# Where a check of the row sums stands in ScalarE's queue, and in which turns later pairs are transposed, in a routing-attention kernel with an MLP behind it

## The chip, the cores and the metric

The kernel runs on one core of a Trainium2 chip. The metric is the device time of one execution in microseconds (us). The kernel before has a median of 1115.66 us over three runs (1114.65 to 1117.67). The profile comes from one further execution of 1114.9 us, whose span from the first to the last instruction is 1113.0 us. PE is TensorE, DVE is VectorE, ACT is ScalarE, POOL is GpSimd, SP issues the DMAs.

## The reference

Four batches of eight heads, 768 positions, head size 64, everything in fp32. A query sees only those keys whose nearest centroid (of 16 for each head) is the same as its own. Then an MLP with a quick GELU over 3072 tokens.

```python
q_assign = argmax(einsum('bhsd,hcd->bhsc', q_n, c_n)); k_assign = ...
mask = q_assign[:, :, :, None] == k_assign[:, :, None, :]
scores = where(mask, scale * q @ k.T, -1e9)
attn = exp(scores - max);  attn = attn / (sum(attn) + 1e-9)
x = (attn @ v) as (B*S, H*D)
h = x @ w_in;  g = h * 1 / (1 + exp(-1.702 * h));  out = g @ w_out
```

## The kernel before, in words

Heads are worked in pairs, since two heads of 64 fill the 128 partitions: 16 pairs, numbered p, four in each batch. Queries are taken in halves of 384, so there are 32 groups g (a pair and a half), and each group has six units u, one for each block of 128 keys. The main loop runs over turns t, two units in a turn, 98 turns in all; three turns (TG) make a group, 24 (TB) a batch.

The order of the work on each engine is the order in which this loop emits it. There is no scheduler that reorders it: an engine takes its instructions one after another and waits at the first that isn't ready. One turn emits:

- `scores` (L392) of its two units on PE, into one of two PSUM buffers named `s`;
- `exps` (L417) on ACT. From the second batch on (turn 24) the result stays in `s`;
- `mask` (L428) on DVE, four instructions, which multiply by the comparison of the cluster codes and write `A`. They also set the `s` buffers free for the scores of the next turn. Then the row sums are added up on POOL (L438);
- `prep_near` (L284 on PE, L290 on ACT), if one is due, and then `values` (L449 on PE) of the turn before; behind a group's last unit ACT copies the result out (L454);
- in every third turn (t = 4, 7, 10, ...) a division, `normalise`: PE adds up the sums (L461), DVE takes the reciprocal (L464) and multiplies (L466). Such a turn is called a division turn here;
- the other steps of preparing a later pair (`prep_at` says in which turn): four transposes in steps 0 to 3 (L270 on PE, L275 on ACT), the nearest centroid, the assignment (L295 on PE, L301 to L324 on DVE), and the spreading of the codes (L331, L336 and two DMAs);
- `check`, two activations on ACT (L476 and L478), which read what the reciprocal wrote and keep two sums; a later test of these sums tells whether the fast path was allowed;
- pieces of the MLP, 0.62 of one in a turn for most of the loop (`first2`, L542, with a GELU at L485 and L486, or `second2`, L491). These fill PE while it would wait for attention.

PSUM has three buffers `m` for everything but scores and values: the transposes, L284, L295, L331, L461, and the MLP. An output of `second2` (`ys`) holds one of them for some eight pieces on end. Behind the loop PE works off the rest of the MLP, at L491 and L700.

Of the kernel before, what the change touches and what calls it, by code (L numbers as in the profile page):

```python
# [38 lines left out]
def fast(  # L39
# [111 lines left out]
    def load_w(i):  # L151
        if i < NW:
            t = wp.tile([P, WN, 2], I32, name="raw")
            nc.sync.dma_start(out=t.rearrange("p n t -> p (n t)"),
                              in_=w_chunks[i][1])
            w_raw[i] = t
# [5 lines left out]
    def split_w(i):  # L162

        hi = w_raw[i][:, :, 1]
        w = w_chunks[i][0]
        e = wp.tile([P, WN], I32, name="e", bufs=2)
        nc.vector.tensor_scalar(out=e, in0=hi, scalar1=EXP, scalar2=None,
                                op0=ALU.bitwise_and)
        nc.vector.tensor_scalar(out=w.bitcast(I32), in0=hi, scalar1=0xFFFFF,
                                scalar2=None, op0=ALU.bitwise_and)  # L170
        nc.scalar.activation(out=e, in_=e, func=AF.Relu, scale=8.0,
                             bias=low[:, 0:1])
        nc.scalar.activation(out=w, in_=w.bitcast(I32), func=AF.Copy,
                             scale=2.0 ** -20, bias=1.0)
        w_pow[i] = e

    def join_w(i):
        raw, e, w = w_raw.pop(i), w_pow.pop(i), w_chunks[i][0]
        nc.vector.scalar_tensor_tensor(
            out=e, in0=raw[:, :, 1], scalar=-2 ** 31, in1=e,  # L180
            op0=ALU.bitwise_and, op1=ALU.bitwise_or)
        nc.vector.scalar_tensor_tensor(
            out=w, in0=raw.bitcast(U32)[:, :, 0], scalar=2.0 ** -52, in1=w,
            op0=ALU.mult, op1=ALU.add)
        nc.vector.tensor_tensor(out=w, in0=w, in1=e.bitcast(FP32),
                                op=ALU.mult)
# [3 lines left out]
    def round_next():  # L190
        i = w_done[0]
        if i < NW:
            load_w(i + 2)
            split_w(i)
        if 0 < i <= NW:
            join_w(i - 1)
        w_done[0] += 1
# [188 lines left out]
    def scores(u):  # L386
        g, kt = divmod(u, NJ)
        p, h = split(g)
        ps = ps_s.tile([P, 2, 512], FP32, name="s")
        for a in range(2):  # L390
            rows = slice(a * D, (a + 1) * D)
            nc.tensor.matmul(out=ps[:, a, 0:HALF],  # L392
                             lhsT=T[p, 1][rows, kt * P:(kt + 1) * P],
                             rhs=T[p, 0][rows, h * HALF:(h + 1) * HALF],
                             start=True, stop=(p >= HP))
        s_of[u] = ps[:, :, 0:HALF]

    def part(u):

        g, kt = divmod(u, NJ)  # L400
        p, h = split(g)
        if p >= HP:
            return
        for a in range(2):
            r = 32 * (2 * (p % 2) + a)
            nc.tensor.matmul(
                out=s_of[u][:, a, :],
                lhsT=hots[p // 2, 1][r:r + NC, kt * P:(kt + 1) * P],
                rhs=hots[p // 2, 0][r:r + NC, h * HALF:(h + 1) * HALF],
                start=False, stop=True)  # L410

    def exps(u):
        p, h = split(u // NJ)
        s = s_of[u]
        if p < HP:
            A_of[u] = ap.tile([P, 2, HALF], FP32, name="A")
        nc.scalar.activation(out=A_of[u] if p < HP else s, in_=s, func=AF.Exp,  # L417
                             scale=SCALE)

    def mask(u):  # L420

        g, kt = divmod(u, NJ)
        p, h = split(g)
        s = s_of.pop(u)
        if p >= HP:
            A_of[u] = ap.tile([P, 2, HALF], FP32, name="A")
            for a in range(2):
                nc.vector.scalar_tensor_tensor(  # L428
                    out=A_of[u][:, a, :],
                    in0=qcode[p][:, a, h * HALF:(h + 1) * HALF],  # L430
                    scalar=code[p][:, kt % NH, 1, kt // NH, a:a + 1],
                    in1=s[:, a, :], op0=ALU.is_equal, op1=ALU.mult)
        A = A_of[u]
        if kt == 0:
            return
        if kt == 1:
            sum_of[g] = ap.tile([P, 2, HALF], FP32, name="sum", bufs=2)
        nc.gpsimd.tensor_tensor(out=sum_of[g],  # L438
                                in0=A_of[u - 1] if kt == 1 else sum_of[g],
                                in1=A, op=ALU.add)  # L440

    def values(u):
        g, kt = divmod(u, NJ)
        p, h = split(g)
        if kt == 0:
            o_of[g] = ps_o.tile([P, 512], FP32, name="o")
        A = A_of.pop(u)
        for a in range(2):
            nc.tensor.matmul(out=o_of[g][a * D:(a + 1) * D, 0:HALF],  # L449
                             lhsT=v_in[p][:, a, kt, :], rhs=A[:, a, :],  # L450
                             start=(kt == 0), stop=(kt == NJ - 1))
        if kt == NJ - 1:
            O_of[g] = xp.tile([P, HALF], FP32, name="x")
            nc.scalar.copy(O_of[g], o_of.pop(g)[:, 0:HALF])  # L454

    def normalise(g):

        sm = sum_of.pop(g)
        ps = bank()
        for a in range(2):  # L460
            nc.tensor.matmul(out=ps[a * D:(a + 1) * D, 0:HALF], lhsT=ones,  # L461
                             rhs=sm[:, a, :], start=True, stop=True)
        rec = recs[g] = short()
        nc.vector.reciprocal(out=rec, in_=ps[:, 0:HALF])  # L464
        x = xT_of[g] = O_of.pop(g)
        nc.vector.tensor_tensor(out=x, in0=x, in1=rec, op=ALU.mult)  # L466
        if g % HP == HP - 1 and g < 2 * HP:
            (half_ffn, ffn)[g // HP].extend((ffn_half, ffn_tiles)[g // HP]())

    recs = {}  # L470

    def check(g):


        rec = recs.pop(g)
        nc.scalar.activation(out=rec, in_=rec, func=AF.Copy,  # L476
                             accum_out=sums[:, 0, g:g + 1])
        nc.scalar.activation(out=rec, in_=rec, func=AF.Relu, bias=top[:, 0:1],  # L478
                             scale=-2.0 * LIMIT * LIMIT,
                             accum_out=sums[:, 1, g:g + 1])  # L480
# [85 lines left out]
    TG = NJ // 2  # L566
    TB = 2 * HP * TG

    prep_at = {}
    for p in range(1, NPAIR):  # L570
        b, hp = divmod(p, HP)
        for i in range(2 if p == 1 else 0, len(PREP)):
            if p == 1:
                t = (i - 2) // 2
            elif b == 0:
                t = (hp - 2) * TG + 1 + i // 2
            else:
                t = b * TB + (-8, -5, -2, 1)[hp] + i
            prep_at.setdefault(t, []).append((p, i))
    loads = deque((p, w) for p in range(NPAIR) for w in range(2))  # L580
    for _ in range(3):
# [2 lines left out]
    def prep(p, i):  # L584
        if i == 0 and p:
            load_v(p)
        PREP[i](p)
        if i in (1, 3) and loads:
            load_qk(*loads.popleft())
# [7 lines left out]
    for t in range(NT + 2):  # L597
        us = range(2 * t, 2 * t + 2) if t < NT else ()
        for u in us:
            scores(u)  # L600
        if t == 0:
            prep(0, 6)
        for u in us:
            part(u)
        for u in us:
            exps(u)
        second_half = t >= TB // 2
        if second_half:
            round_next()
        for u in us:  # L610
            mask(u)
        work = sorted(prep_at.get(t, ()), key=lambda w: PREP[w[1]] != prep_near)
        while work and PREP[work[0][1]] == prep_near:
            prep(*work.pop(0))
        if 1 <= t <= NT:
            for u in range(2 * t - 2, 2 * t):
                values(u)

        todo = half_ffn or (ffn if len(ffn) > NF // 2 else ())
        owed += (rate if half_ffn else 0.62) if todo else -owed  # L620
        g = (t - 2) // TG if t >= 2 and (t - 2) % TG == TG - 1 else None
        if g is not None and second_half:
            normalise(g)
        for p, i in work:
            prep(p, i)
        if g is not None and not second_half:
            normalise(g)
        if recs:
            check(*recs)
        if second_half or t and t % 4 != 3:  # L630
            round_next()
        while owed >= 1 and todo:
            todo.popleft()()
            owed -= 1
        if second_half and t % 2:
            round_next()
    qcode.clear()
    att.close()

# [561 lines left out]
```

## Time and profile before

| | us |
|---|---|
| median of three runs (1114.65 to 1117.67) | 1115.66 |
| profiled execution | 1114.9 |
| its span | 1113.0 |
| PE busy | 1039.0 (93%) |
| DVE busy | 603.0 (54%) |
| ACT busy | 359.5 (32%) |
| POOL busy | 295.9 (27%) |

The span falls into three stretches: batch 0 up to about 227 us, batches 1 to 3 (turns 24 to 97) up to about 633 us, and then the rest of the MLP. In the last stretch, from 633 to 1113, PE is busy for 474.24 of 480 us. "Idle" in a row is the time for which the engine stood still just before the instruction, and the arrow names what it waited for. A matmul in fp32 shows up as two instructions in the profile, so four matmuls of the kernel are x8 there.

### The profile page before, as it was taken

The page shows a single profiled execution, that of the slowest core. Times are in us where ns is not written, and L with a number is a line of the kernel's source. Part 1 is how long each engine was busy: PE and PEld are TensorE (multiplying, and loading weights), DVE is VectorE, ACT ScalarE, POOL GpSimd, SP SyncE. Part 2 cuts the span into 40 slices and gives each one's busy share as a digit, 9 for nine tenths or more (in the row PEclk, how much of TensorE's full clock was granted, in tenths as well). Part 3 has the DMA queues.
Part 4 walks back from the last instruction along what each step waited for, and adds up shares of the span by engine and source line. Part 5 has one row for each costly group of instructions (what it writes and reads, how often), then busy time and mean ns, then how long its engine had stood idle before and what let it go on. Part 6 is the DMA issues. An engine that isn't in the chain of part 4 may idle for free. (4 is left out here: it accounts for less than half of the span.)

```text
span 1113.0 us, 11101 instructions
## 1 busy us (share of the span) xinstructions
PE 1039.0 (93%) x4142; PEld 503.9 (45%) x4142; DVE 603.0 (54%) x912; ACT 359.5 (32%) x649; POOL 295.9 (27%) x168
## 2 busy tenths in 40 slices
PE   7878799999899998999897899999999999999997
PEld 4323354445434354444453355544455444555443
DVE  3889998237666786677776676600166300465000
ACT  4654555224435544554453212200022100122000
POOL 2554231215465555655565300000000000000000
PEclk9989899999989999999998999999999999999999
DMA  7423443211002310131000000000000000000000
GB/s 202 126 75 96 145 143 105 60 45 46 8 15 57 95 42 3 29 92 39 8 1 0 1 10 0 1 19 19 19 0 1 10 19 19 9 1 1 20 19 21
DMA packets 64816, 45.17 MB, mean 41 GB/s; under 512 B 51952, under 2 KB 57584, under 8 KB 64752
## 3 DMA queue, kind: packets, MB, share of 16 engines
q1 hardware_dynamic: 64608, 44.33, 13.9%
q8 instruction: 35, 0.57, 0.2%
q14 instruction: 29, 0.24, 0.1%
q10 hardware_dynamic: 144, 0.03, 0.0%
HBM read 38.04 MB, written 6.31 MB: 40 GB/s over the span
## 5 line engine op out<-in xcount | busy, mean ns | idle before, releaser
L438 POOL TENSOR_TENSOR sum<-sum,A 128x768 f32<-128x768 f32 x128 | 235.7, 1841 | 252.3 <-DVE A L428 153.4
L491 PE MATMUL m<-w_out,gb 128*128 128x512 f32 x576 | 247.7, 592 | 0.0
L428 DVE SCALAR_TENSOR_TENSOR A<-qb,code,s 128x384 f32<-128x384 uint8 x288 | 158.3, 610 | 125.5 <-ACT s L417 109.7
L705 DVE TENSOR_TENSOR gb<-b,gb 128x384 f32<-128x384 f32 x168 | 93.4, 557 | 213.8 <-PE b L700 207.2
L392 PE MATMUL s<-T,T 64*128 64x384 f32 x768 | 165.3, 542 | 35.6 <-DVE A L428 21.1
L491 PEld LDWEIGHTS m<-w_out,gb 128*128 128x128 f32 x576 | 109.4, 190 | 137.1 <-issue 136.6
L449 PE MATMUL o<-A,inv 128*64 128x384 f32 x768 | 154.1, 523 | 3.6 <-DVE A L428 3.6
L417 ACT ACTIVATE s<-s 128x768 f32<-128x768 f32 x144 | 109.5, 788 | 58.8 <-PE s L392 57.2
L392 PEld LDWEIGHTS s<-T,T 64*128 64x128 f32 x768 | 68.0, 195 | 113.5 <-issue 38.3
L496 ACT ACTIVATE y<-m 128x512 f32<-128x512 f32 x24 | 14.3, 597 | 257.0 <-PE m L491 243.9
L485 ACT ACTIVATE th<-gb 128x768 f32<-128x768 f32 x48 | 40.4, 843 | 170.1 <-DVE gb L705 140.3
L449 PEld LDWEIGHTS o<-A,inv 128*64 128x64 f32 x768 | 49.1, 142 | 94.0 <-issue 87.9
L464 DVE RECIPROCAL short<-m 128x384 f32<-128x384 f32 x32 | 81.7, 2552 | 12.7 <-PE m L461 12.7
L438 POOL TENSOR_TENSOR sum<-A 128x768 f32<-128x768 f32 x32 | 58.8, 1839 | 77.9 <-ACT A L417 41.7
L700 PE MATMUL b<-x,S 128*128 128x384 f32 x192 | 69.8, 486 | 0.0
L700 PE MATMUL b<-T,w_in 128*128 128x384 f32 x192 | 69.8, 486 | 0.0
L700 PE MATMUL b<-x,w_in 128*128 128x384 f32 x192 | 66.3, 486 | 0.0
L513 PE MATMUL m<-x,w_in 128*128 128x384 f32 x128 | 49.6, 543 | 13.3 <-ACT T L275 4.5
L486 DVE SCALAR_TENSOR_TENSOR gb<-th,gb 128x768 f32<-128x768 f32 x48 | 45.8, 954 | 21.8 <-ACT th L485 21.8
L491 PE MATMUL m<-w_out,g 128*128 128x512 f32 x120 | 56.8, 597 | 0.0
L542 PEld LDWEIGHTS m<-x,w_in 128*128 128x128 f32 x384 | 44.7, 192 | 10.7 <-issue 10.6
L476 ACT ACTIVATE short<-short 128x384 f32<-128x384 f32 x32 | 16.7, 523 | 100.8 <-DVE x L466 100.8
(95 smaller groups left out, 898.5 us busy)
## 6 DMA issues: line engine op xcount, KB each, us to landing
raw<-in_moe_w_in_dram SPq DMA_DIRECT2D x16, 512.0 KB
raw<-in_moe_w_out_dram SPq DMA_DIRECT2D x16, 512.0 KB
in<-in_q_dram SPq DMA_DIRECT2D x32, 192.0 KB
in<-in_k_dram SPq DMA_DIRECT2D x32, 192.0 KB
inv<-in_v_dram SPq DMA_DIRECT2D x16, 384.0 KB
out_dram<-y SPq DMA_DIRECT2D x24, 256.0 KB
qb<-line SPq DMA_DIRECT2D x12, 192.0 KB
line<-row SPq DMA_DIRECT2D x12, 1.5 KB
```

The costliest lines, as they stand in the source:

```text
L392: nc.tensor.matmul(out=ps[:, a, 0:HALF], lhsT=T[p, 1][rows, kt * P:(kt + 1) * P], rhs=T[p, 0][rows, h * HALF:(h + 1) * HALF], start=True, ...
L417: nc.scalar.activation(out=A_of[u] if p < HP else s, in_=s, func=AF.Exp, scale=SCALE)
L428: nc.vector.scalar_tensor_tensor(out=A_of[u][:, a, :], in0=qcode[p][:, a, h * HALF:(h + 1) * HALF], scalar=code[p][:, kt % NH, 1, kt // NH ...
L438: nc.gpsimd.tensor_tensor(out=sum_of[g], in0=A_of[u - 1] if kt == 1 else sum_of[g], in1=A, op=ALU.add)
L449: nc.tensor.matmul(out=o_of[g][a * D:(a + 1) * D, 0:HALF], lhsT=v_in[p][:, a, kt, :], rhs=A[:, a, :], start=(kt == 0), stop=(kt == NJ - 1))
L464: nc.vector.reciprocal(out=rec, in_=ps[:, 0:HALF])
L486: nc.vector.scalar_tensor_tensor(out=g, in0=t, scalar=1.0, in1=h, op0=ALU.add, op1=ALU.mult)
L491: nc.tensor.matmul(out=ps[:, 0:DM], lhsT=g, rhs=w_out[:, f, :], start=(f == 0), stop=(f == NF - 1))
L513: nc.tensor.matmul(out=ps[:, 0:HALF], lhsT=w_in[:, c, f * P:(f + 1) * P], rhs=xT[c], start=(c == 0), stop=(c == NCH - 1))
L542: nc.tensor.matmul(out=ps[:, f % 2 * P:(f % 2 + 1) * P], lhsT=w_in[:, c, f * P:(f + 1) * P], rhs=xT[c][:, n * P:(n + 1) * P], start=(c == ...
L700: nc.tensor.matmul(out=ps[:, 0:HALF], lhsT=a(c), rhs=x(c), start=(c == 0), stop=(c == 1))
L705: nc.vector.tensor_tensor(out=o, in0=a, in1=b, op=ALU.add)
```

## The change

Two things, both by place alone; no instruction is added or taken away. From turn 24 the check of a division turn is not emitted at the end of that turn but in the next turn, between `exps` and `mask`; the last one stands behind the loop. And the transposes of the pairs of batches 1 to 3 move: for a pair whose first group starts in turn T they stood in turns T-8, T-7, T-6 and T-5, one each, of which T-8 and T-5 are division turns; now there are two in T-7 and two in T-6. The other three steps stay in T-4, T-3 and T-2.

```diff
@@ -575,7 +575,7 @@
             elif b == 0:
                 t = (hp - 2) * TG + 1 + i // 2
             else:
-                t = b * TB + (-8, -5, -2, 1)[hp] + i
+                t = b * TB + TG * hp - (7, 7, 6, 6, 4, 3, 2)[i]
             prep_at.setdefault(t, []).append((p, i))
@@ -607,6 +607,8 @@
         if second_half:
             round_next()
+        if recs:
+            check(*recs)
         for u in us:
             mask(u)
@@ -625,7 +627,7 @@
         if g is not None and not second_half:
             normalise(g)
-        if recs:
+        if recs and t < TB:
             check(*recs)
@@ -634,6 +636,7 @@
         if second_half and t % 2:
             round_next()
+    check(*recs)
     qcode.clear()
     att.close()
```

ACT's queue in a division turn of batch 1, and in the two turns behind it, where no transposes are due (L417 is `exps`, L485 the GELU of an MLP piece, L454 the copy of a group's result). Before:

```order
L476 ACTIVATE short,sums<-short 128x384
L478 ACTIVATE short,sums<-short,top 128x384
L417 ACTIVATE s<-s 128x2x384 x2
L485 ACTIVATE g<-m 128x256
L417 ACTIVATE s<-s 128x2x384 x2
L454 COPY x<-o 128x384
L485 ACTIVATE g<-m 128x256
```

The same place now:

```order
L417 ACTIVATE s<-s 128x2x384 x2
L476 ACTIVATE short,sums<-short 128x384
L478 ACTIVATE short,sums<-short,top 128x384
L485 ACTIVATE g<-m 128x256
L417 ACTIVATE s<-s 128x2x384 x2
L454 COPY x<-o 128x384
L485 ACTIVATE g<-m 128x256
```

The two rows of the check have moved behind one pair of `exps`; what stands behind them is as it was.

PE's queue from a division turn on (its L461 to the first L491), through the next turn and the one behind that, where a pair is being prepared. Before:

```order
L461 MATMUL m<-sum,ones 64x384 x2
L331 LDWEIGHTS qc
L331 MATMUL m<-ident_h,qc 12x128
L270 MATMUL m<-ident,in 128x128 x6
L491 MATMUL m<-w_out,g 128x512 x2
L392 MATMUL s<-T_1666,T_1767 128x384 x4
L284 MATMUL m<-T_2318,cT 32x384 x2
L284 MATMUL m<-T_2398,cT 32x384 x2
L449 MATMUL o<-A,inv 64x384 x4
L270 MATMUL m<-ident,in 128x128 x3
L392 MATMUL s<-T_2213,T_2275 128x384 x4
L449 MATMUL o<-A,inv 64x384 x4
```

The same place now, from L331 to the second turn's transposes:

```order
L331 LDWEIGHTS qc
L331 MATMUL m<-ident_h,qc 12x128
L491 MATMUL m<-w_out,g 128x512 x2
L392 MATMUL s<-T_1706,T_1767 128x384 x4
L284 MATMUL m<-T_2349,cT 32x384 x2
L284 MATMUL m<-T_2398,cT 32x384 x2
L449 MATMUL o<-A,inv 64x384 x4
L270 MATMUL m<-ident,in 128x128 x6
L392 MATMUL s<-T_2237,T_2275 128x384 x4
L449 MATMUL o<-A,inv 64x384 x4
L295 MATMUL m<-ident,short 128x128 x3
L270 MATMUL m<-ident,in 128x128 x6
```

The two steps of transposes (x3 each) that stood behind L331 are gone from the division turn; the next two turns have two steps each instead of one, the second pair of them behind L295.

## Rows read from the trace of the kernel before

**Rows 1.** The page, busy time of each engine (share of the span) and instructions.

```profile
PE 1039.0 (93%) x4142; PEld 503.9 (45%) x4142; DVE 603.0 (54%) x912; ACT 359.5 (32%) x649; POOL 295.9 (27%) x168
```

**Rows 2.** Who PE waited for, 227 to 633 us: total, times, longest.

```profile
PE s L392 <- DVE A L428: 21.1, 11, 4.2
PE m L270 <- ACT T L275: 4.0, 7, 0.6
PE o L449 <- DVE A L428: 3.6, 1, 3.6
PE s L392 <- ACT g L485: 2.1, 3, 0.8
PE m L270 <- ACT row L336: 1.7, 5, 0.3
```

**Rows 3.** Groups of instructions, 227 to 623 us: busy, mean ns, idle before.

```profile
L476 ACT ACTIVATE short<-short 128x384 f32<-128x384 f32 x24 | 12.6, 523 | 73.7 <-DVE x L466 73.7
...
L478 ACT ACTIVATE short<-short,top 128x384 f32<-128x384 f32 x24 | 14.8, 615 | 0.8
```

**Rows 4.** Timeline of one division and the turns behind it: start, duration, idle before.

```profile
413.73 1.56 PE L392 MATMUL s<-T,T 64*128 64x384 f32 x8
...
414.02 2.55 DVE L464 RECIPROCAL short<-m 128x384 f32<-128x384 f32 x1
...
416.60 0.71 DVE L466 TENSOR_TENSOR x<-x,short 128x384 f32<-128x384 f32 x1
...
416.66 2.05 PE L542 MATMUL m<-x,w_in 128*128 128x128 f32 x16
417.35 0.52 ACT L476 ACTIVATE short<-short 128x384 f32<-128x384 f32 x1 [3.25 <-DVE x L466]
...
418.61 1.48 ACT L417 ACTIVATE s<-s 128x768 f32<-128x768 f32 x2
419.50 2.19 DVE L428 SCALAR_TENSOR_TENSOR A<-qb,code,s 128x384 f32<-128x384 uint8 x4 [2.19 <-ACT s L417]
...
420.78 1.97 PE L392 MATMUL s<-T,T 64*128 64x384 f32 x8 [2.07 <-DVE A L428]
...
426.10 1.56 PE L392 MATMUL s<-T,T 64*128 64x384 f32 x8
```

**Rows 5.** Timeline of PE, 264 to 300 us.

```profile
288.25 2.48 PE L392 MATMUL s<-T,T 64*128 64x384 f32 x8 [2.21 <-DVE A L428]
...
295.21 1.56 PE L392 MATMUL s<-T,T 64*128 64x384 f32 x8
```

**Rows 6.** PE's granted clock (behind POOL) in two stretches of it.

```profile
290.80:294.50 3.70, 3.70 (x19) 1.89 (x20) 1.61 (x3) 1.27 (x2) 2.65 (x2) 0.71 0.00 0
294.50:299.00 4.50, 4.50 (x29) 2.27 (x30) 2.30 (x5) 1.88 (x3) 0.90 (x2) 1.00 0.01 2
```

**Rows 7.** Timeline of two late turns without MLP pieces.

```profile
607.79 2.93 PE L392 MATMUL s<-T,T 64*128 64x384 f32 x8 [4.18 <-DVE A L428]
...
623.77 3.35 PE L449 MATMUL o<-A,inv 128*64 128x384 f32 x8 [3.57 <-DVE A L428]
```

**Rows 8.** Timeline of two turns without an MLP piece between their scores.

```profile
436.88 1.97 PE L392 MATMUL s<-T,T 64*128 64x384 f32 x8 [2.19 <-DVE A L428]
...
440.22 1.81 PE L392 MATMUL s<-T,T 64*128 64x384 f32 x8
```

**Rows 9.** Timeline of a division turn with transposes, and the turn behind it.

```profile
490.04 0.55 PE L270 MATMUL m<-ident,in 128*128 128x128 f32 x3 [0.34 <-ACT row L336]
...
491.15 0.55 PE L270 MATMUL m<-ident,in 128*128 128x128 f32 x3 [0.57 <-ACT T L275]
...
495.92 0.48 ACT L290 COPY short<-m 128x384 f32<-128x384 f32 x1
...
497.06 0.55 PE L270 MATMUL m<-ident,in 128*128 128x128 f32 x3
```

## The prediction

> **What bounds the kernel now.** I read the page first: PE is busy for 93% of the span, the other engines for a third to a half [rows 1]. So only PE's idle time is to be had, and whatever slows its clock. The view of the chain that ended last is of no use here: it ends in the last output's copy and is one step long. The second view was who PE waited for while attention of batches 1 to 3 runs: the largest entries are scores (L392) that wait for masks (L428), 21.1 us in 11 waits, then values (L449) that wait for masks, 3.6 in one wait, transposes (L270), 4.0 and 1.7, and scores behind a GELU, 2.1 [rows 2]. The third view, groups of instructions, shows ACT standing for 73.7 us in 24 waits at the check's first activation, each time until DVE's multiplication L466 is through [rows 3]. ACT has time enough, so this wait costs only by what is queued behind it, and the timeline shows that.
>
> In the turn of 414 us DVE takes the reciprocal from 414.02 to 416.57 and multiplies to 417.31 [rows 4]. PE issued the scores of the next turn at 413.73, 1.56 us, and they were done by 415.3. But ACT's next instruction is the check: it waits 3.25 us, runs from 417.35, and only at 418.61 do the exponentials of those scores begin. The masks follow at 419.50, after DVE has stood for 2.19 us. PE ends its MLP piece at 416.66 + 2.05 = 418.71 and stands for 2.07 us until the first mask has freed an `s` buffer; the next scores start at 420.78. So in a division turn a check that nobody needs soon holds back exponentials, masks and scores.
>
> **The check.** Behind the change the exponentials are ahead of the check. Their scores are ready at 415.3, and two of them take 1.48 us [rows 4], so they end at about 416.9, while DVE is still at the multiplication. The masks can start when DVE is free, at 417.35 instead of 419.50: 2.15 us earlier. The next scores could then start at 420.78 - 2.15 = 418.63, and PE comes to them at 418.71: the stall of 2.07 is gone, and what is late next is PE itself.
>
> How much of each stall goes is the smaller of the stall and 2.15. The three entries that the check causes add up to 21.1 + 3.6 + 2.1 = 26.8 us [rows 2]; the GELU one belongs to them since that GELU stands behind the check in ACT's queue. Two stalls are longer: 4.18 at 607.79 keeps 2.03, and 3.57 at 623.77 keeps 1.42, both late in the loop where no MLP piece is left [rows 7]. A few others lie slightly over 2.15, such as the 2.21 at 288.25 [rows 5]; I put these at 0.35 in all. Term 1: 26.8 - 2.03 - 1.42 - 0.35 = 23.0 us.
>
> Behind such a stall the pair of scores takes 1.97 instead of 1.56 us, because its second unit waits for a mask of its own [rows 4]. There are 14 such scores (11 and 3 waits, rows 2). I take half, since in turns without an MLP piece the loop of scores, exponentials and masks sets the pace anyway: 440.22 - 436.88 = 3.34 us from scores to scores [rows 8], and that stays. Term 2: 7 x 0.41 = 2.9 us (bounds 0 and 14 x 0.41 = 5.7).
>
> The check itself, 418.61 - 417.35 = 1.26 us, costs nothing if it is done before the next exponentials are due. It starts at 417.35 as before, once L466 is through; the next scores start at 418.7 and take some 0.8 for a unit, so the exponentials are due at 419.6, a microsecond after the check's end. Queued behind the check are now the copies of L284 and of transposes, the GELU of that turn's piece and those exponentials. If that cover went, it would cost up to 1.26 us in each of 24 turns, 30 us. The check of the last group moves behind the loop, with nothing late behind it: 0.
>
> **PE's clock.** The stall of 2.21 us at 288.25 is followed by a stretch of a granted clock of 0.71 on the mean, from 290.8 to 294.5, and then 1.00 again [rows 6]: for part of that stretch the lower level, 1.2 GHz. From these scores to the next, with an MLP piece between, it took 295.21 - 288.25 = 6.96 us [rows 5]; the same distance without a fall took 426.10 - 420.78 = 5.32 [rows 4]. A fall costs 1.64 us. I count seven falls, the first at 288.25 and the last at 623.77; five follow stalls that should vanish, two follow the late ones that only shrink. Upper bound 7 x 1.64 = 11.5, lower bound 0 (falls that come anyway, from the waits that are left). Five would give 8.2; I take term 3 as 6.
>
> The Trainium skill (TensorE: Matmul & The Clock Gate, section What's actually happening) says that the throttled clock is the default and activity lifts it; by that a vanished stall takes its fall along, 8.2 us, and without it the term would be 0. The trace agrees only in part: the stall of 2.07 at 420.78 had no fall behind it [rows 4].
>
> **The transposes.** Twelve pairs have them moved. In a division turn with `ys` held and the division's sums in a second buffer, one `m` buffer is left: the first transposes wait 0.34 for the copy of L331's result, the second 0.57 for the copy of the first [rows 9]. In total 1.7 and 4.0 us [rows 2]. The 0.34 goes, since L331 is alone now. The 0.57 recurs: in the turn of L295 its buffer is kept by DVE, `ys` by PE, and two transposes share one buffer again. In the turn ahead, the second transposes wait for L284's copy, which stands behind exponentials and check together, as before, and ends at 495.92 + 0.48 = 496.40; PE comes there at about 497.06 - 0.91 + 0.49 = 496.64, so no wait [rows 9]. On SP's queue the loads that steps 0 and 3 issue move by a turn with them: the values' load to one turn later, the next load of q to one turn earlier and so ahead of the codes' two DMAs (L338, L340). Each is needed three or more turns later, and no wait in rows 2 names a DMA, so I put this at nothing; held-up codes would stop the masks at a pair's start. Term 4: 1 us of gain. Bounds: 5.7 gained, or, if all 24 second transposes wait 0.57, 13.7 - 5.7 = 8 lost.
>
> The Trainium skill (Perfetto Trace Analysis, section Optimization Strategy) holds that a gap that repeats can mean too little PSUM for the next tile. By that rule moving them would give nothing, as long as there are three buffers; I lean that way, the 0.34 apart.
>
> **The sum.** 23.0 + 2.9 + 6 + 1 = 32.9 us. Against the profiled execution: 1114.9 - 32.9 = 1082.0. The median shown is 0.8 above that execution, so 1083.
>
> **The rivals.**
> *The clock does not come back.* The stalls go, but short waits still bring as many falls: 1083 + 6 = 1089. For it: not every stall has a fall, so what sets them off isn't the stall alone.
> *The next limit is near.* Half of terms 1 to 3 comes back as other waits, because DVE now goes from multiplication to masks without a pause and the 3.34 us loop governs more turns [rows 8]: 1083 + 16 = 1099. Against it: in most turns an MLP piece of 2 us stands on PE and covers the loop.
> *It does not do what it says.* DVE or POOL would have held the masks anyway: 1115. Against it: DVE's 2.19 of idle time ends with the exponentials [rows 4].
> *Slower.* ACT, now held at the check while copies stand behind it, delays the copies of two transposes in one turn, so that PE waits at each of 24 second transposes for the check and a copy, 1.26 + 0.57 = 1.83 us, 44 in all: 1083 + 44 = 1127. It decides from 1.4 us each, where 24 waits eat the 33 us. Against it: the copy's place worked out above.
>
> **Chances.** Forecast 0.60 (its own range 1076 to 1088), clock 0.12, next limit 0.17, no effect 0.06, slower 0.05. A difference of under 0.3% (3.3 us) can't be told from no change here; so faster 0.89, same 0.06, slower 0.05. The range leaves out the two last and half of the next limit, and at the low end what lies beyond some 40 us: 1075 to 1099.
>
> **What would show it.** In the profile after: no wait of scores for masks of about 2 us behind an MLP piece, and L417 ahead of L476 in each division; ACT's wait at L476 shorter than 73.7 us; masks that start right behind L466; granted clock 1.00 from 280 to 600 us; the span of batches 1 to 3 some 33 us shorter and the stretch behind it as long as before. Wrong would be a new wait of L270 or L295 for ACT of over 10 us, or scores that now wait as long for exponentials.

## The result, and the profile after

The changed kernel takes 1081.95 us, the median of four runs (1081.31 to 1083.81), against 1115.27 before on the same chip (four runs, 1114.65 to 1117.67): a ratio of 0.970 with a 95% interval of 0.968 to 0.972. The prediction was 1083. The profiled execution took 1083.81 us with a span of 1082.0, against 1114.9 and 1113.0.

The page of the kernel after, the row that answers to [rows 1]:

```profile
PE 1030.4 (95%) x4142; PEld 503.5 (47%) x4142; DVE 600.2 (55%) x912; ACT 359.6 (33%) x649; POOL 295.6 (27%) x168
```

No engine has less to do: the instructions are as many as before, and of the busy times only PE's is shorter by much, 8.6 us, since its matmuls run less often at the lower clock. The other 22 of the 31 us were idle time of PE.

Who PE waited for after, 220 to 603 us (total, times, longest):

```profile
PE m L270 <- ACT T L275: 2.8, 5, 0.6
PE m L461 <- POOL sum L438: 2.2, 1, 2.2
PE s L392 <- DVE A L428: 2.2, 3, 1.7
PE m L270 <- ACT short L290: 1.1, 1, 1.1
PE o L449 <- DVE A L428: 1.1, 1, 1.1
```

Against [rows 2] the scores' wait for masks has gone from 21.1 to 2.2 us, that of the values from 3.6 to 1.1, and the scores' wait behind a GELU is not there any more. One entry is new, the 1.1 us of transposes (L270) behind L290's copy. At the end of the loop PE's sums (L461) wait 2.2 us for POOL; that wait stood in the kernel before too, as the entry that follows the five of [rows 2] (227 to 633 us):

```profile
PE m L461 <- POOL sum L438: 1.3, 1, 1.3
```

ACT's own wait at the check is still there, but short (groups of instructions, 220 to 600 us: busy, mean ns, idle before; [rows 3] had 73.7):

```profile
L476 ACT ACTIVATE short<-short 128x384 f32<-128x384 f32 x24 | 12.6, 524 | 12.9 <-DVE x L466 12.9
```

One division of the kernel after, to be laid beside [rows 4] (start, duration, idle before):

```profile
401.59 1.56 PE L392 MATMUL s<-T,T 64*128 64x384 f32 x8
...
402.01 2.55 DVE L464 RECIPROCAL short<-m 128x384 f32<-128x384 f32 x1
...
402.60 1.50 ACT L417 ACTIVATE s<-s 128x768 f32<-128x768 f32 x2 [0.65 <-PE s L392]
...
404.52 2.05 PE L542 MATMUL m<-x,w_in 128*128 128x128 f32 x16
404.59 0.71 DVE L466 TENSOR_TENSOR x<-x,short 128x384 f32<-128x384 f32 x1
405.22 2.17 DVE L428 SCALAR_TENSOR_TENSOR A<-qb,code,s 128x384 f32<-128x384 uint8 x4
405.33 0.52 ACT L476 ACTIVATE short<-short 128x384 f32<-128x384 f32 x1 [1.23 <-DVE x L466]
...
406.50 1.96 PE L392 MATMUL s<-T,T 64*128 64x384 f32 x8
```

The exponentials (L417) run while DVE still takes the reciprocal, the masks start with the end of the multiplication (405.22, where L466 ends at 405.30), and PE goes from the MLP piece to the next scores without standing. Before, 4.12 us lay between the starts of L542 and of these scores (416.66 to 420.78); now 1.98. The scores still take 1.96 us, though nothing holds their start.

A window of the kernel after (its length; busy time of PE, PEld, DVE, ACT, POOL; granted clock, share of DMA, GB/s):

```profile
227.00:600.00 373.00, 360.95 (x1989) 172.72 (x1988) 275.42 (x418) 186.45 (x352) 217.33 (x120) 1.00 0.14 36
```

From 227 to 600 us PE is busy for 97% at a granted clock of 1.00 on the mean; before it was busy for 91% of 227 to 633 us, at 0.97 (a fall, below, is a stretch in which the granted clock is 0.50, the lower of its two levels):

```profile
227.00:633.00 406.00, 370.73 (x1983) 174.34 (x1980) 277.72 (x419) 186.02 (x352) 217.41 (x120) 0.97 0.13 33
```

A finer measure than the whole time is the distance from one group's reciprocal (L464) to the next, since each group has one. In groups 0 to 5 (batch 0) these distances differ by up to 5 us in sum between executions of one and the same kernel; from group 7 on they repeat to a few hundredths nearly everywhere. From group 7's reciprocal to group 31's it was 629.33 - 240.57 = 388.76 us before and 596.79 - 244.58 = 352.21 after: 36.6 us gained. Of that 4.0 are lost up to group 7's (244.58 against 240.57; group 6 alone took 42.51 instead of 37.77) and 1.5 behind group 31's, which leaves the 31.0 by which the span fell. So the change contains a loss, in batch 0's last turns. Group 6's own length shows it best: in a second execution of the changed kernel group 7's reciprocal came at 240.41, by the spread of the groups ahead, but group 6 took 42.27 again. The experiments take it apart.

### The profile page after: what moved, and what is told of

Same layout as the page of the kernel before. It is cut to its first block, busy times and chain, and to the rows that moved or that the text cites. A ratio compares the mean times of both kernels' runs of the same rounds, so it can differ in the third digit from the quotient of the medians.

```text
span 1082.0 us, 11138 instructions
## 1 busy us (share of the span) xinstructions
PE 1030.4 (95%) x4142; PEld 503.5 (47%) x4142; DVE 600.2 (55%) x912; ACT 359.6 (33%) x649; POOL 295.6 (27%) x168
## 3 DMA queue, kind: packets, MB, share of 16 engines
q1 hardware_dynamic: 64608, 44.33, 14.3%
## 5 line engine op out<-in xcount | busy, mean ns | idle before, releaser
L491 PE MATMUL m<-w_out,gb 128*128 128x512 f32 x576 | 247.7, 592 | 0.0
L491 PEld LDWEIGHTS m<-w_out,gb 128*128 128x128 f32 x576 | 109.4, 190 | 137.1 <-issue 136.6
L392 PE MATMUL s<-T,T 64*128 64x384 f32 x768 | 159.2, 527 | 13.1 <-ACT A L417 9.0
L449 PE MATMUL o<-A,inv 128*64 128x384 f32 x768 | 148.3, 506 | 1.1 <-DVE A L428 1.1
L417 ACT ACTIVATE s<-s 128x768 f32<-128x768 f32 x144 | 109.3, 793 | 83.2 <-PE s L392 72.0
L496 ACT ACTIVATE y<-m 128x512 f32<-128x512 f32 x24 | 14.3, 596 | 261.9 <-PE m L491 238.9
L485 ACT ACTIVATE th<-gb 128x768 f32<-128x768 f32 x48 | 40.4, 842 | 170.0 <-DVE gb L708 140.0
L464 DVE RECIPROCAL short<-m 128x384 f32<-128x384 f32 x32 | 81.7, 2552 | 14.7 <-PE m L461 14.6
L491 PE MATMUL m<-w_out,g 128*128 128x512 f32 x120 | 59.0, 616 | 0.2 <-ACT T L275 0.2
L542 PEld LDWEIGHTS m<-x,w_in 128*128 128x128 f32 x384 | 44.7, 192 | 11.2 <-issue 10.2
L542 PE MATMUL m<-x,w_in 128*128 128x128 f32 x384 | 48.8, 280 | 0.5 <-ACT T L275 0.5
```

The source lines that it names most:

```text
L392: nc.tensor.matmul(out=ps[:, a, 0:HALF], lhsT=T[p, 1][rows, kt * P:(kt + 1) * P], rhs=T[p, 0][rows, h * HALF:(h + 1) * HALF], start=True, ...
L449: nc.tensor.matmul(out=o_of[g][a * D:(a + 1) * D, 0:HALF], lhsT=v_in[p][:, a, kt, :], rhs=A[:, a, :], start=(kt == 0), stop=(kt == NJ - 1))
L491: nc.tensor.matmul(out=ps[:, 0:DM], lhsT=g, rhs=w_out[:, f, :], start=(f == 0), stop=(f == NF - 1))
L542: nc.tensor.matmul(out=ps[:, f % 2 * P:(f % 2 + 1) * P], lhsT=w_in[:, c, f * P:(f + 1) * P], rhs=xT[c][:, n * P:(n + 1) * P], start=(c == ...
```

## The experiments

A time is a median with its lowest and highest run; "group 6" is the distance from group 5's reciprocal to group 6's, and "loop" that from group 7's to group 31's, both in the profiled execution. The kernel before took 1114.56, 1115.44 and 1115.34 us in the three sessions (8 to 11 runs each), beside the first four experiments, the next four and the last three.

| kernel | us | ratio, 95% interval | group 6 | loop |
|---|---|---|---|---|
| before | | | 37.77 | 388.76 |
| changed | 1081.95 (1081.31 to 1083.81) | 0.970 (0.968 to 0.972) | 42.51 | 352.21 |
| check alone | 1080.38 (1079.22 to 1081.22) | 0.970 (0.968 to 0.971) | 37.73 | 353.57 |
| transposes alone | 1124.63 (1123.23 to 1125.17) | 1.009 (1.007 to 1.011) | 42.30 | 394.42 |
| batch 1's pairs at their old turns | 1076.40 (1076.15 to 1081.28) | 0.968 (0.966 to 0.970) | 37.73 | 353.79 |
| check of the group before | 1081.29 (1079.16 to 1083.24) | 0.971 (0.969 to 0.972) | 37.73 | 355.73 |
| check behind the reciprocal | 1095.96 (1093.41 to 1099.29) | 0.983 (0.981 to 0.986) | 37.74 | 371.72 |
| check at the next turn's end | 1078.73 (1074.73 to 1080.69) | 0.967 (0.965 to 0.969) | 37.74 | 352.86 |
| no check | 1077.02 (1072.93 to 1079.65) | 0.965 (0.963 to 0.967) | 37.74 | 353.02 |
| before, its stalls filled | 1103.46 (1101.86 to 1104.87) | 0.990 (0.988 to 0.992) | 37.73 | 378.93 |
| checks behind exponentials from turn 12 | 1081.04 (1080.09 to 1082.90) | 0.970 (0.968 to 0.971) | 38.58 | 353.23 |
| changed, again | 1081.68 (1079.19 to 1084.21) | 0.970 (0.968 to 0.972) | 42.27 | 352.47 |
| batch 1's at old turns, again | 1078.49 (1076.56 to 1081.15) | 0.966 (0.964 to 0.968) | 37.75 | 353.41 |

### The two parts apart

Check alone: the changed kernel with the transposes where they were.

```diff
-                t = b * TB + TG * hp - (7, 7, 6, 6, 4, 3, 2)[i]
+                t = b * TB + (-8, -5, -2, 1)[hp] + i
```

> The check moved, the transposes where they were before. Theory (the wait in ACT's queue is the whole gain): about 1080 us, so even slightly under the changed kernel's 1082, since the changed kernel lost some 4 us in batch 0 between 164 and 207 us, where only transposes moved, and won back 2 us at most by them later. Rival (the division turn was overloaded, the transposes did a good part): 1095 us or more.

Transposes alone: the same edit the other way round, in the kernel before.

> The transposes moved, the check where it was before. Theory: 1117 us or so, the 4 us of batch 0 lost and 1 to 2 us of waits for L331's copy won. Rival (transposes did a good part): 1100 us or less.

The check brings 1114.56 - 1080.38 = 34.2 us, more than the whole change. The transposes alone cost 10.1 us. Neither expectation had that number: the waits cost far more than was put on them. The view of PE's waits of this kernel, 120 to 633 us, shows where:

```profile
PE s L392 <- DVE A L428: 22.8, 13, 4.2
PE m L270 <- ACT short L290: 5.4, 5, 2.6
PE m L513 <- DVE short L464: 5.4, 1, 5.4
PE m L513 <- ACT short L290: 4.9, 1, 4.9
```

The rows with L290 add up to 10.3 us; in the kernel before PE waits for L290 once in this window, 2.2 us. One of these waits, on the timeline of the same kernel:

```profile
517.79 0.52 ACT L476 ACTIVATE short<-short 128x384 f32<-128x384 f32 x1 [3.26 <-DVE x L466]
...
519.05 1.48 ACT L417 ACTIVATE s<-s 128x768 f32<-128x768 f32 x2
...
520.46 0.48 ACT L290 COPY short<-m 128x384 f32<-128x384 f32 x1
...
521.00 0.90 PE L270 MATMUL m<-ident,in 128*128 128x128 f32 x3 [2.56 <-ACT short L290]
```

The second transposes of a turn need the buffer that L290's copy empties, and that copy stands behind the check and the exponentials. So the two parts depend on each other: with the check moved, four of the five waits in the loop are gone and the fifth is 1.1 us.

### Batch 1's pairs at their old turns

```diff
+            elif b == 1:
+                t = b * TB + (-8, -5, -2, 1)[hp] + i
             else:
                 t = b * TB + TG * hp - (7, 7, 6, 6, 4, 3, 2)[i]
```

> The changed kernel, but the four pairs of batch 1, whose transposes fall into the last turns of batch 0, keep their old turns. Theory (the 4.9 us wait at 179 us comes from two transposes in one turn whose PSUM buffers wait for a copy that ACT does late): 1078 us, and the reciprocals of groups 5 to 7 stand where they stood before. Rival (that stretch varies from run to run, or the check does it): 1082 us as with the change.

1076.40 us, and 1078.49 in another session beside the changed kernel's 1081.68. That repeat was to show 3 to 5 us with intervals that don't meet; it shows 3.2, and the intervals overlap at the edge. The traces are plainer. Group 6 takes 37.73 us again, not 42.51. The changed kernel's timeline shows what that group's turns hold:

```profile
173.65 0.87 PE L270 MATMUL m<-ident,in 128*128 128x128 f32 x6
...
174.30 3.77 POOL L438 TENSOR_TENSOR sum<-sum,A 128x768 f32<-128x768 f32 x2 [6.82 <-ACT A L417]
174.49 1.91 DVE L167 TENSOR_SCALAR e<-raw 128x512 int32<-128x512 int32 x1
176.32 2.02 DVE L169 TENSOR_SCALAR w_out<-raw 128x512 int32<-128x512 int32 x1
...
178.38 0.63 ACT L173 ACTIVATE w_out<-w_out 128x512 f32<-128x512 int32 x1 [1.22 <-DVE w_out L169]
...
178.92 0.46 ACT L290 COPY short<-m 128x384 f32<-128x384 f32 x1
...
179.43 2.93 PE L513 MATMUL m<-x,w_in 128*128 128x384 f32 x4 [4.91 <-ACT short L290]
```

The same turn of the kernel before:

```profile
173.76 0.55 PE L270 MATMUL m<-ident,in 128*128 128x128 f32 x3
...
174.14 2.75 PE L513 MATMUL m<-x,w_in 128*128 128x384 f32 x8
...
179.05 3.61 PE L513 MATMUL m<-x,w_in 128*128 128x384 f32 x7 [2.17 <-ACT short L290]
```

DVE still splits weights there (L167, L169), ACT waits for it (L173), and L290's copy waits behind that. Before, one block of transposes took one buffer and an MLP piece had another: PE stood for 2.17 us. Now two blocks of transposes (x6) take both, the MLP piece gets none, and PE stands for 4.91. That is 2.7 of the 4.7 us; another 1.0 is a wait of the second transposes behind L295, at 195.33 us, for DVE (L304), which the kernel before doesn't have in group 6.

With batch 1's pairs put back, batches 2 and 3 still have the new turns, and from group 7's reciprocal to group 24's this kernel takes 264.58 us, as the check alone does (264.54); up to group 25's it is 279.33 against 279.77. So there the new turns are worth at most 0.4 us, and in batch 1 they cost 4.7 us in group 6 and give 1.7 back in groups 7 to 9. By the traces this version is 3.0 us faster than the changed kernel; the medians differ by as much, but the single runs overlap (1076.56 to 1081.15 and 1079.19 to 1084.21).

### Is it the check's wait, its place or its work?

Check of the group before: the check stays at its old place, ahead of the next turn's exponentials, but takes the sums of one division earlier.

```diff
-        if recs:
-            check(*recs)
+        if recs and (t < TB or len(recs) > 1):
+            check(min(recs))
```

(and a last `check(*recs)` behind the loop)

> The kernel before, with the check at its old place in the division turn, but from turn 24 for the group before, so that its input has long been there; the same work on ACT ahead of the same exponentials, but no wait. Theory (the wait for the multiplication is what costs): 1080 to 1085 us, as with the check moved. Rival (the 1.3 us of work ahead of the exponentials costs too): 1095 us or more.

1081.29 us: as good as moving the check. On its timeline the check runs without a wait, and the exponentials behind it end before DVE is through with the multiplication at 399.01:

```profile
395.52 0.52 ACT L476 ACTIVATE short<-short 128x384 f32<-128x384 f32 x1
...
395.71 2.55 DVE L464 RECIPROCAL short<-m 128x384 f32<-128x384 f32 x1
...
396.77 1.48 ACT L417 ACTIVATE s<-s 128x768 f32<-128x768 f32 x2
...
398.30 0.71 DVE L466 TENSOR_TENSOR x<-x,short 128x384 f32<-128x384 f32 x1
398.93 2.17 DVE L428 SCALAR_TENSOR_TENSOR A<-qb,code,s 128x384 f32<-128x384 uint8 x4
...
400.21 1.96 PE L392 MATMUL s<-T,T 64*128 64x384 f32 x8
```

So it is the wait in front of the exponentials, not the check's 1.26 us nor its place as such. The loop is 2.2 us longer than with the check moved (355.73 and 353.57); 1.65 of this lies in group 30 (13.49 and 11.84), where the granted clock is 0.50 from 574.8 to 578.2 us, a fall that the kernel with the check moved doesn't have.

Check behind the reciprocal: in the kernel before, the check's two activations write elsewhere, so that they wait for the reciprocal alone and not for the multiplication, which reads the same buffer.

```diff
-        nc.scalar.activation(out=rec, in_=rec, func=AF.Copy,
+        to = (rec if 3 * g + 4 < TB else
+              hot.rearrange("p a c -> p (a c)").bitcast(FP32))
+        nc.scalar.activation(out=to, in_=rec, func=AF.Copy,
...
```

> The kernel before, with the check at its old place, but from turn 24 it writes its throw-away result to another tile, so that it waits for the reciprocal only and no longer for the multiplication behind it (0.7 us). Theory (each stall shrinks by as much as the exponentials come earlier, here 0.7 us): 14 stalls by 0.5 to 0.7 each, 8 to 9 us, and up to 5 more where the clock stays up: 1100 to 1107 us. Rival (a stall goes all at once or not at all): 1114 or 1082 us.

1095.96 us, some 4 us faster than the lower end expected. The waits came out a little shorter than expected: the three entries of 26.8 us are down to 17.1 (this one and 2.8 of the values), 9.7 less where 8 to 9 were expected. What PE's scores waited, 227 to 633 us:

```profile
PE s L392 <- DVE A L428: 14.3, 12, 3.2
```

Scores waited 14.3 us instead of 21.1, a stall behind a division 1.33 us instead of 2.07. What the expectation missed most is the clock: from 227 to 585 us the granted clock rounds to 1.00, and only three falls were left: one behind a stall of 1.45 us at 424.86, where the granted clock is 0.76 from 424.8 to 432 and group 19 takes 15.02 us instead of some 13.4 (before's 14.11 less the 0.74 by which the stall is shorter), and two behind the late stalls near 590 and 604.

No check: the kernel with batch 1's pairs at their old turns, and the checks of groups 7 to 31 left out, their sums set to 0. (Those sums and the test on them are the part of the computation that is missing.)

```diff
         if recs:
-            check(*recs)
+            recs.clear()
...
```

> The same with the checks of groups 7 to 31 left out (their sums stay at zero), which is part of the computation. Theory (at its new place the check's 1.3 us lie under PE's work): within 2 us of the kernel with the check, 1074 to 1077 us. Rival (the cover is partial): 0.5 to 1.2 us less in each of 24 turns, 1048 to 1064 us.

1077.02 us, between the two medians of the same kernel with checks (1076.40 and 1078.49); the loop takes 353.02 us instead of 353.79 and 353.41. On the whole, then, the checks, 27 us of work on ACT [rows 3], cost 0.4 to 0.8 us. Two things that cancel are in this: without them group 24 takes 16.54 us instead of 17.88, since a wait of transposes for L290 is gone, and group 30 takes 13.48 instead of 11.84, since the clock falls there (0.51 from 575.1 to 578.5 us), as it does in neither execution of the kernel with checks. Without that fall the checks would cost some 2 us. The cover holds for the rest.

Check at the next turn's end, in the same kernel, behind that turn's transposes and copies (`due = tuple(recs)` ahead of them, `check(*due)` behind):

> The changed kernel with the pairs of batch 1 at their old turns, and the check at the end of the next turn instead of right behind the exponentials. It differs only in turns with transposes, where the copies of L284 and of two transposes now stand ahead of the check. Theory (the check delays L284's copy and with it the second transposes, 1.1 us once): that wait of L270 for L290 is gone, 1075 to 1077 us. Rival (the check delays these copies in more places than the waits of PE show): 1072 us or less.

1078.73 us: no gain that can be told. The wait for L290 is gone from PE's list, as expected, and group 24 takes 16.54 us instead of 17.88, but group 30 takes 13.49 instead of 11.84, with a fall of the clock (0.50 from 576.3 to 579.7 us). The loop is 0.6 to 0.9 us shorter.

Checks behind the exponentials from turn 12 on, in the same kernel (`if recs and t < TB // 2` at the old place):

> The changed kernel with the pairs of batch 1 at their old turns (as in e3), and the checks behind the next exponentials from turn 12 instead of 24. Theory (the wait at the check delays whatever stands behind it on ACT, in batch 0 too, where ACT waits 27 of its 101 us): 2 to 5 us less than e3. Rival (in batch 0 DVE splits the MLP's weights and sets the pace, so that ACT's wait costs nothing there): within 1.5 us of e3.

1081.04 us, beside 1078.49 for the same kernel with the checks moved from turn 24: no gain. Group 6 took 38.58 us instead of 37.73. In batch 0 the check isn't what holds PE.

### What the clock is worth

The kernel before, with matmuls that nothing uses (transposes of the identity, 150 in all) at the end of nine turns with a long stall:

```diff
+    FILL = {32: 14, 35: 14, 38: 14, 56: 14, 59: 14, 80: 14, 89: 14, 92: 28,
+            95: 24}
...
+        if t in FILL:
+            ps = bank()
+            for _ in range(FILL[t]):
+                nc.tensor.transpose(out=ps[:, 0:P], in_=ident, identity=ident)
```

> The kernel before, with transposes of the identity matrix, that nobody reads, put on PE behind the nine turns with the longest stalls (14 of them, some 1.8 us; 28 and 24 behind the two long ones), so that PE stands still for a short time only while all waits of the other engines stay. Theory (a fall of the clock costs 1.6 us and follows the stall): no fall left there, 1103 to 1106 us. Rival (the falls have another cause, or the clock costs nothing): 1114 us or more.

1103.46 us, 12.0 under the kernel before, with more work on PE and with ACT waiting at the check as long as ever. A division of this kernel:

```profile
408.77 0.52 ACT L476 ACTIVATE short<-short 128x384 f32<-128x384 f32 x1 [3.26 <-DVE x L466]
...
409.98 1.69 PE L642 MATMUL m<-ident 128*128 128x128 f32 x14
410.04 1.48 ACT L417 ACTIVATE s<-s 128x768 f32<-128x768 f32 x2
410.93 2.19 DVE L428 SCALAR_TENSOR_TENSOR A<-qb,code,s 128x384 f32<-128x384 uint8 x4 [2.19 <-ACT s L417]
...
412.21 1.96 PE L392 MATMUL s<-T,T 64*128 64x384 f32 x8 [0.55 <-DVE A L428]
```

The masks come as late as before (2.19 us of DVE's idle time), so no score comes earlier; the filler (L642) only keeps PE at work. And the clock stays up for the whole loop (window as above; before, 0.97):

```profile
227.00:615.00 388.00, 368.84 (x2103) 183.18 (x2101) 270.37 (x409) 183.41 (x347) 216.19 (x120) 1.00 0.13 34
```

One fall is left just behind the loop (0.51 from 615.8 to 619.3 us). Groups that had a fall behind their stall became shorter, such as group 10, 17.75 to 16.10 us, and groups that had none did not (group 18: 16.10 and 16.11). In the loop it adds up to 388.76 - 378.93 = 9.8 us; the other 2 of the 12.0 lie within the spread of batch 0. The part that doesn't need the clock is seen where no fall was: groups 18 and 19 gain 2.28 us each from the change, groups 10 and 11 gain 3.94 and 3.71.

## Why the prediction was right, and where not

**The mechanism was right, and shown.** The check's wait, by what is queued behind it on ACT, held masks and scores. Taking away the wait alone, at the old place, gives nearly the same as moving it (1081.29 and 1080.38; 2.2 us more in the loop, most of it one fall of the clock); shortening it by the multiplication gives a part. The stall at a division went whole, as worked out.

**Term 1, 23.0 us.** Three entries added up to 26.8 [rows 2]; with the check moved 3.3 are left (2.2 and 1.1, where 3.8 were expected). That is 23.5. But at the loop's end the wait of L461 for POOL, which the sum did not look at, grew from 1.3 to 2.2 us: 22.6.

**Term 2, 2.9 us: too large.** Half of 14 scores were to fall back from 1.97 to 1.56 us. In the kernel after 11 still take 1.95 to 1.97, such as the one at 406.50 above: their second unit waits for its mask even where the first doesn't (there it starts at 407.55, and the masks end at 405.22 + 2.17 = 407.39). So 3 x 0.41 = 1.2.

**Term 3, 6 us: too small.** The step that failed was to take less than five falls of seven, because one stall of 2.07 had none behind it, and to leave the two late ones standing. Filling the stalls gives 9.8 in the loop, six of the seven falls are gone after (the one left lies at the loop's end), and the price of one was right: 3.94 - 2.28 = 1.66 and 3.71 - 2.28 = 1.43 us against 1.64. The bound above, 11.5, was the better end. The rule of the Trainium skill that the prediction weighed (TensorE: Matmul & The Clock Gate, section What's actually happening), that activity lifts a clock that is throttled by default, would have given 8.2; the filled kernel agrees with its direction (granted clock 1.00 from 227 to 615 us). The one fall that is left in the kernel after lies behind the last waits, 1.1 us of the values and 2.2 of L461 (windows: length, busy times of PE, PEld, DVE, ACT, POOL, granted clock):

```profile
591.00:595.00 4.00, 2.44 (x8) 0.77 (x8) 1.58 (x4) 1.32 (x5) 2.96 (x2) 1.00 0.01 2
595.00:600.00 5.00, 4.30 (x9) 1.73 (x10) 3.10 (x3) 0.00 (x0) 0.65 (x1) 0.66 0.00 0
```

Terms 1 to 3 were to give 31.9 us; the check alone gives 34.2, and 35.2 in the loop. The terms as measured are 22.6 + 1.2 + 9.8 = 33.6; the other 1.6 of the 35.2 I can't put to a row. A part is that PE's start without a wait lies 0.07 us ahead of the end of the instruction before it (404.52 + 2.05 = 406.57, and the scores start at 406.50), about 1 us in 14 stalls.

**Term 4, 1 us of gain: the wrong sign.** It is a loss of 4.7 - 1.7 = 3.0 us, all in batch 1's pairs, and next to nothing in batches 2 and 3. Two steps failed. The prediction read one division turn of the middle batches [rows 9] for all twelve pairs, but batch 1's are prepared while batch 0 runs, where L290's copy stands behind activations that wait for the weights' splitting. And "so no wait" for the second transposes behind L284's copy holds for four of five waits; one of 1.13 us is left. Its working took off the two waits that go, 0.34 and 0.57, but not the two blocks of transposes that leave the division turn with them (0.55 us each, [rows 9]), so PE comes there about 1 us sooner than the 496.64 it gave. On the timeline of the kernel after:

```profile
493.52 0.52 ACT L476 ACTIVATE short<-short 128x384 f32<-128x384 f32 x1 [1.11 <-DVE x L466]
...
494.79 0.46 ACT L290 COPY short<-m 128x384 f32<-128x384 f32 x1
...
495.30 0.55 PE L270 MATMUL m<-ident,in 128*128 128x128 f32 x3 [1.13 <-ACT short L290]
...
501.87 0.55 PE L270 MATMUL m<-ident,in 128*128 128x128 f32 x3 [0.57 <-ACT T L275]
```

There the check, ahead of the copy, is what makes it late: this is the slower rival's mechanism in one place of 24. The 0.57 recurs five times, 2.8 us in all, and the 0.34 is gone, both as predicted. The Trainium skill (Perfetto Trace Analysis, section Optimization Strategy) holds that a gap that repeats can mean too little PSUM for the next tile. The trace agrees as far as it goes: with as many buffers as before, the wait moved and stayed (4.0 us in 7 before, 2.8 in 5 after). No run had a fourth buffer, so that the buffers are the cause, here and in group 6, is read from the kernel and the waits.

**The sum** came out at 31.1 us between the two profiled executions (1114.9 - 1083.81) against 32.9: a term too large by 1.7 (the second), one too small by 3.8 (the third), a wrong sign worth 4.0, a wait that grew by 0.9, the 1.6 without a row and the 1.5 behind the loop, where the last fall lies, partly cancel. (With the check alone, which has no fall there, the stretch behind group 31's reciprocal is 483.8 us, as before, 483.7.) That the time was hit more closely than its parts is luck.

**What stays open.** What sets off a fall of the clock: stalls of 2.07 to 2.26 us mostly had one behind them, but not those at 420.78 and 436.88 [rows 4, 8]; with the check behind the reciprocal one of 1.45 had one, and others of 1.33 to 1.52 had none; with the check of the group before one of 1.68 at 573.36 had one, with the check moved one of 1.73 at 576.79 had none. The versions with the check moved and batch 1's pairs in their old turns can't be ranked among themselves by time (1076.40 to 1080.38), since batch 0's spread is as large; where that spread comes from wasn't tried.

## What to carry to other kernels

An engine that is a third busy can still set the time by where it waits: look at what is queued behind an instruction that waits for something nobody needs soon, and put the work that others wait for ahead of it, or let the waiting instruction take data that have been there for a while. A short stall of TensorE may cost nearly twice its length, by the clock behind it (here some 2.2 us, and 1.4 to 1.7 more). When a change moves work by a table, read the turns at the table's edges, not only one in the middle.

## What the runs showed of the hardware that was not expected

- Matmuls that nothing uses, put where PE would stand, made the kernel before 12.0 us faster (ratio 0.990, interval 0.988 to 0.992).
- DVE's L167 and L169, operations on one tile in SBUF that take 0.42 us alone, took 1.91 and 2.02 us beside POOL's additions (174.30 to 178.07). The Trainium skill (SBUF — State Buffer, section Who interferes with whom) says that such an operation can take a pair of ports that DVE shares with GpSimd, and that the one that issues first holds it for its whole instruction while the other blocks. These rows agree: POOL's addition starts first each time, L167 and L169 end at 176.40 and 178.34, and POOL's two additions of some 1.9 us each at about 176.1 and at 178.07.
- From group 7 on, the distances between reciprocals of one kernel repeat in two executions: 263.50 and 263.51 us from group 7 to group 24 of the changed kernel. What differs between runs is nearly all in batch 0.
